# Grouped-query attention: V of the second K/V unit asked for ahead of its K, and VectorE's share of the exponentials also in chunk 3

## The chip, the cores and the metric

One core of one Trainium2 chip. The metric is the device time of one execution in microseconds (us). The span of the profile, from the first instruction to the last, is 1.6 to 1.8 us shorter than the device time. Three words recur: a transfer is *issued* when SyncE begins to put it into its queue (the profile gives how long that holds SyncE), it *lands* when its last byte is announced, and the *fill* is the first 12 us or so, until TensorE runs without a gap.

## The reference

Softmax attention in bfloat16, 16 batches, 32 query heads on 8 K/V heads (4 query heads share one), 288 queries, 512 keys, 128 columns per head:

```python
B, Hq, Hkv, Sq, Sk, D = 16, 32, 8, 288, 512, 128
scores = jnp.einsum("bhqd,bhkd->bhqk", q, k) * scale
p = _softmax(scores, axis=-1)
return jnp.einsum("bhqk,bhkd->bhqd", p, v)
```

## The kernel before

A group is one K/V head of one batch with its 4 x 288 = 1152 queries: 128 groups. A group is cut into 3 chunks of 1536 columns of transposed scores, so 384 chunks. For chunk n TensorE makes the scores (`ps_s`), ScalarE their exponentials (`pt_sb`), TensorE, two chunks behind, the product with V (`ps_o`), with a column of ones that gives the row sums, and VectorE divides and evicts (`rl_sb`, `o_sb`). In a "shared" chunk, each sixth one, VectorE makes 120 of the 1536 exponentials with a bit trick and a polynomial: `y`, `t`, `m`, `e`, three times `u`, and the result into `pt_sb`, eight operations in all.

```python
    UG = 4                      # groups in one K/V unit: one transfer of K and one of V for four groups
    SHARED = list(range(2 * NC, NS - NC, EVERY)) + [NS - NC]      # NC = 3, EVERY = 6, NS = 384
    ...
        def op_k(u, g0=0, g1=UG):                                 # K: a transposing transfer
            ...
            eng.dma_start_transpose(
                kt_sb[:, sl, :, g0:g1].rearrange("d j g p -> d j (g p)"),
                k_v[(u * UG + g0) * P:(u * UG + g1) * P]
            ).then_inc(sem["us_k%d" % sl if u > 0 else "s_k%d" % g0], 16)
    ...
        def op_vc(g):                    # GpSimd copies V beside the column of ones
            eng = nc.gpsimd
            waits = [have("v", g)]
            if g >= 2:
                waits.append(("s_pv", NC * (g - 2) + 2))
            emit(eng, waits, lambda: eng.tensor_copy(
                v_sb[:, sl, gi * NJ:(gi + 1) * NJ, 0:D], vd_sb[:, sl, gi].rearrange("p (j d) -> p j d", d=D))
            ).then_inc(sem["s_vc"], 1)
    ...
        first = [lambda: op_q0(0), lambda: op_v(0, None, 0, 1)]
        first += [lambda: op_q(1), lambda: op_k(0, 1, 2), lambda: op_v(0, None, 1, 2), lambda: op_k(0, 2),
                  lambda: op_q(2), lambda: op_v(0, None, 2, UG), lambda: op_q(3)]
        sp = []                          # the order in which SyncE issues the rest: sorted by t
        for u in range(1, NU):
            t = max(NC * UG * (u - NSLOT + 1) + 0.5, NC * (UG * u - 2.5) / AHEAD - 0.2)
            sp.append((t, lambda u=u: op_k(u)))
            sp.append((t + (2.0 if u >= NSLOT else 0.35), lambda u=u: op_v(u)))
        for g in range(UG, NG):
            t = max(NC * (g - NQ + 1) + 1.2, NC * (g - 2.5) / AHEAD)
            sp.append((t, lambda g=g: op_q(g)))
        ...
        sp.sort(key=lambda x: x[0])
    ...
            for n in range(NS):          # TensorE
                op_s(n)
                if shared(n):
                    op_sy(n)
                if n >= LAG:             # LAG = 2
                    op_pv(n - LAG)
```

All loads and stores but the first K go through SyncE's one queue. Unit 1 (groups 4 to 7) is first needed by the scores of chunk 12 (K, and Q of group 4) and by the output matmuls of chunk 12 (V, after GpSimd's copy).

Of the kernel before, what the change touches and what calls it, by code (L numbers as in the profile page):

```python
# [131 lines left out]
def bass_standalone__gqa_softmax__near_ridge_kernel(  # L132
# [19 lines left out]
    NC = COLS // CH  # L152
# [10 lines left out]
    EVERY = 6  # L163
# [5 lines left out]
    NSLOT = 3  # L169
# [6 lines left out]
    NO = 12  # L176
    NS = NG * NC
    LASTG = NG - 1
    SHARED = list(range(2 * NC, NS - NC, EVERY)) + [NS - NC]
    FINE = NG - 2  # L180
    ALONE = 8 * TPC

# [7 lines left out]
    with ExitStack() as es:  # L190
# [72 lines left out]
        def need(eng, waits):  # L263

            left = []
            for (s, n) in waits:
                key = (id(eng), s)
                if seen.get(key, 0) < n:
                    seen[key] = n
                    left.append((sem[s], n))  # L270
            return left
# [15 lines left out]
        def op_k(u, g0=0, g1=UG):  # L287
            eng = nc.sync
            sl = u % NSLOT
            if u >= NSLOT:  # L290
                for (s, n) in need(eng, [("s_s", NC * UG * (u - NSLOT + 1))]):
                    eng.wait_ge(s, n)
# [5 lines that stand above are left out]
        def op_v(u, eng=None, g0=0, g1=UG):  # L298
            eng = eng or nc.sync
            sl = u % NSLOT  # L300
            if u >= NSLOT:
                for (s, n) in need(eng, [("s_vc", UG * (u - NSLOT + 1))]):
                    eng.wait_ge(s, n)
            eng.dma_start(
                vd_sb[:, sl, g0:g1], v_v[:, u * UG + g0:u * UG + g1]
            ).then_inc(sem["us_v%d" % sl if u > 0 else "s_v%d" % g0], 16)
# [222 lines left out]
        def shared(n):  # L529
            return n in SHARED  # L530

        def nth(n):
            return SHARED.index(n) + 1

# [104 lines left out]
        sp = []  # L639
        for u in range(1, NU):  # L640
            t = max(NC * UG * (u - NSLOT + 1) + 0.5, NC * (UG * u - 2.5) / AHEAD - 0.2)
            sp.append((t, lambda u=u: op_k(u)))
            sp.append((t + (2.0 if u >= NSLOT else 0.35), lambda u=u: op_v(u)))
        for g in range(UG, NG):
            t = max(NC * (g - NQ + 1) + 1.2, NC * (g - 2.5) / AHEAD)
            sp.append((t, lambda g=g: op_q(g)))
# [124 lines left out]
```

## Time and profile before

| | |
|---|---|
| time, median of 3 runs | 521.99 us (521.82 to 522.11) |
| profiled execution | 521.84 us, span 520.2 us |
| busy: TensorE, ScalarE, VectorE, GpSimd | 99%, 99%, 71%, 15% |
| chain that ended last | TensorE 97% of the span |
| distance between chunks in the steady part | 1.33 us, for TensorE and ScalarE alike |

The page gives busy time and share per engine. The chain of waits gives, in order of time, the pieces of work that the end depended on. The timeline gives start, length, engine, line, operation, output<-inputs, shape, count, and in brackets the idle time before it and what ended that. The lines that carry the argument stand in the prediction. Two more are needed for all comparisons below, because they separate the start from the rest: the first exponential and the last reciprocal of VectorE, from the timeline of the kernel before:

```profile
4.84 1.08 ACT L521 ACTIVATE pt_sb<-ps_s 128x512 bf16<-128x512 f32 x2 [2.11 <-PE ps_s L449]
...
517.27 0.17 DVE L585 RECIPROCAL rl_sb<-ps_s 128x3 f32<-128x3 f32 x1
```

The time between them, 517.27 - 4.84 = 512.43 us, I call **the stretch**. It doesn't count the moment at which the first Q landed. It isn't wholly free of it, though: the later transfers don't wait for the first exponential, so a late start gives them a lead over the computing.

### The profile page before, as it was taken

The page shows a single profiled execution, that of the slowest core. Times are in us where ns is not written, and L with a number is a line of the kernel's source. Part 1 is how long each engine was busy: PE and PEld are TensorE (multiplying, and loading weights), DVE is VectorE, ACT ScalarE, POOL GpSimd, SP SyncE. Part 2 cuts the span into 40 slices and gives each one's busy share as a digit, 9 for nine tenths or more (in the row PEclk, how much of TensorE's full clock was granted, in tenths as well). Part 3 has the DMA queues.
Part 4 walks back from the last instruction along what each step waited for, and adds up shares of the span by engine and source line. Part 5 has one row for each costly group of instructions (what it writes and reads, how often), then busy time and mean ns, then how long its engine had stood idle before and what let it go on. Part 6 is the DMA issues. An engine that isn't in the chain of part 4 may idle for free.

```text
span 520.2 us, 15366 instructions
## 1 busy us (share of the span) xinstructions
PE 516.2 (99%) x6226; PEld 394.6 (76%) x6226; DVE 370.5 (71%) x1322; ACT 513.4 (99%) x393; POOL 79.8 (15%) x135
## 2 busy tenths in 40 slices
PE   9999999999999999999999999999999999999997
PEld 5777777777777777777777777777777777777776
DVE  2767767777777677676776776767767767777777
ACT  7999999999999999999999999999999999999997
POOL 1111111111111111111111111111111111111110
PEclk9999999999999999999999999999999999999999
DMA  8999999899999998999999999999999999998212
GB/s 167 211 234 269 257 206 250 213 205 223 212 228 263 220 240 203 225 240 240 223 235 211 201 235 215 246 191 190 230 241 238 230 205 184 198 216 221 84 69 93
DMA packets 253782, 110.06 MB, mean 212 GB/s; under 512 B 220304, under 2 KB 237584, under 8 KB 253712
## 3 DMA queue, kind: packets, MB, share of 16 engines
q1 hardware_dynamic: 253568, 108.95, 99.5%
q8 instruction: 49, 0.80, 0.7%
q14 instruction: 21, 0.17, 0.1%
q10 hardware_dynamic: 144, 0.13, 0.1%
HBM read 16.91 MB, written 37.75 MB: 105 GB/s over the span
## 4 chain that ended last, share of the span: by engine, by line
PE 97%; DVE 2%; ACT 1%; issue 0%
PE ps_o L489 49%; PE ps_s L449 46%; PE ps_o L460 1%; ACT pt_sb L521 1%; ACT pt_sb L526 1%; PE ps_o L427 0%; DVE o_sb L595 0%; DVE u_sb L559 0%; DVE rl_sb L585 0%; DVE m_sb L550 0%; PE ps_s L427 0%; DVE pt_sb L566 0%; PE ps_o L414 0%; DVE t_sb L543 0%; DVE o_sb L605 0%
## 5 line engine op out<-in xcount | busy, mean ns | idle before, releaser
L526 ACT ACTIVATE pt_sb<-ps_s 128x1536 bf16<-128x1536 f32 (+2 forms) x384 | 508.2, 1438 | 0.1
L489 PE MATMUL ps_o<-v_sb,pt_sb 128*128 128x129 bf16 x4584 | 322.6, 220 | 0.1
L489 PEld LDWEIGHTS ps_o<-v_sb,pt_sb 128*128 128x128 bf16 x4584 | 282.6, 98 | 50.2 <-DVE o_sb L595 14.1
L449 PE MATMUL ps_s<-qt_sb,kt_sb 128*128 128x512 bf16 (+2 forms) x1536 | 308.9, 324 | 0.2
L595 DVE TENSOR_TENSOR o_sb<-ps_o,rl_sb 128x384 bf16<-128x384 f32 x382 | 211.7, 554 | 8.8
L449 PEld LDWEIGHTS ps_s<-qt_sb,kt_sb 128*128 128x128 bf16 x1536 | 123.6, 98 | 61.9 <-ACT pt_sb L526 0.7
L585 DVE RECIPROCAL rl_sb<-ps_o 128x3 f32<-128x3 f32 x382 | 67.8, 178 | 128.6 <-PE ps_o L489 127.2
L578 POOL COPY v_sb<-vd_sb 128x512 bf16<-128x512 bf16 x128 | 78.8, 616 | 429.2 <-PE ps_o L489 407.6
L559 DVE SCALAR_TENSOR_TENSOR u_sb<-u_sb,m_sb 128x120 f32<-128x120 f32 x128 | 36.2, 283 | 2.2
L566 DVE SCALAR_TENSOR_TENSOR pt_sb<-u_sb,e_sb 128x120 bf16<-128x120 f32 x64 | 18.1, 283 | 2.3
L559 DVE SCALAR_TENSOR_TENSOR u_sb<-m_sb 128x120 f32<-128x120 f32 x64 | 17.7, 276 | 0.0
L537 DVE TENSOR_SCALAR y_sb<-ps_o 128x120 f32<-128x120 f32 x64 | 16.2, 253 | 0.0
L550 DVE TENSOR_SCALAR m_sb<-t_sb 128x120 int32<-128x120 int32 x64 | 14.6, 228 | 2.2
L460 PE MATMUL ps_o<-qt_sb,kt_sb 128*128 128x120 bf16 x64 | 13.8, 216 | 0.0
L550 DVE TENSOR_SCALAR e_sb<-t_sb 128x120 int32<-128x120 int32 x64 | 13.8, 216 | 0.0
L543 DVE TENSOR_SCALAR t_sb<-y_sb 128x120 int32<-128x120 f32 x64 | 13.7, 214 | 0.0
L460 PEld LDWEIGHTS ps_o<-qt_sb,kt_sb 128*128 128x128 bf16 x64 | 6.3, 98 | 7.7 <-DVE o_sb L595 0.3
L521 ACT ACTIVATE pt_sb<-ps_s 128x512 bf16<-128x512 f32 (+1 forms) x6 | 4.3, 748 | 2.1 <-PE ps_s L449 2.1
L621 DVE TENSOR_REDUCE st_sb<-rl_sb 128x1 f32<-128x72 f32 (+1 forms) x16 | 3.4, 215 | 0.0
L623 DVE TENSOR_REDUCE st_sb<-rl_sb 128x1 f32<-128x72 f32 (+1 forms) x16 | 3.4, 215 | 0.0
L427 PE MATMUL ps_o<-const-bfloat16-1.0 128*128 128x512 bf16 (+1 forms) x6 | 2.4, 573 | 0.9 <-PEq L756 0.9
L685 ACT ACT_TABLE_LOAD x1 | 1.3, 1283 | 1.2 <-PEq L756 1.2
(32 smaller groups left out, 11.7 us busy)
## 6 DMA issues: line engine op xcount, KB each, us to landing
out_dram<-o_sb SPq DMA_DIRECT2D x126, 288.0 KB, 4.0
vd_sb<-in_v_dram SPq DMA_DIRECT2D x31, 512.0 KB, 5.4
qt_sb<-in_q_dram SPq DMA_TRANSPOSE x128, 5.1
out_dram<-o_sb SPq DMA_DIRECT2D x6, 96.0 KB, 1.8
kt_sb<-in_k_dram SPq DMA_TRANSPOSE x33, 5.1
vd_sb<-in_v_dram SPq DMA_DIRECT2D x2, 128.0 KB, 3.0
vd_sb<-in_v_dram SPq DMA_DIRECT2D x1, 256.0 KB, 3.5
kd_sb<-in_k_dram ACTq DMA_DIRECT2D x1, 128.0 KB, 2.3
```

The source lines that it names most:

```text
L449: ins = emit(eng, w_x, lambda: eng.matmul(ps_s[:, n % 2, c:c + w], kt_sb[:, sl, j, gi, :], qg[:, t * P:t * P + w], start=True, stop=True))
L460: emit(eng, [("s_ev", n - LAG - 1)], lambda: eng.matmul(ps_o[:, (n - LAG) % 2, BANK - W:BANK], kt_sb[:, (g // UG) % NSLOT, j, g % UG, :], ...
L489: ins = emit(eng, w_x, lambda: eng.matmul(outs(r)[:, t - r % NC * TPC, :], pt(g, t, j), v_sb[:, sl, gi * NJ + j, 0:DV], start=(x == 0), st ...
L526: emit(eng, waits, lambda: eng.activation(d, s, ACTF.Exp, scale=scale)).then_inc(sem["s_e"], 1)
L537: emit(eng, [("s_yb", nth(n) - NB), ("s_pv", n - LAG + 1)], lambda: eng.tensor_scalar(out=y_sb[:, b], in0=ps_o[:, (n - LAG) % 2, BANK - W: ...
L543: emit(eng, [("s_ym", 2 * (nth(n) - NB)), ("s_y", nth(n))], lambda: eng.tensor_scalar(out=t_sb[:, b], in0=y_sb[:, b], scalar1=Y_MUL, scala ...
L550: emit(eng, [("s_yp", nth(n) - NB), ("s_yb", nth(n))], lambda: eng.tensor_scalar(out=dst[:, b], in0=t_sb[:, b], scalar1=mask, scalar2=bits ...
L559: lambda: eng.scalar_tensor_tensor(out=u_sb[:, b, x], in0=src, scalar=QUARTIC[x], in1=m, op0=ALU.add, op1=ALU.mult)
L566: lambda: eng.scalar_tensor_tensor(out=pt_sb[:, n % NPT, CH - W:CH], in0=u_sb[:, b, 2], scalar=QUARTIC[3], in1=e_sb[:, b].bitcast(FP32), o ...
L578: emit(eng, waits, lambda: eng.tensor_copy(v_sb[:, sl, gi * NJ:(gi + 1) * NJ, 0:D], vd_sb[:, sl, gi].rearrange("p (j d) -> p j d", d=D))). ...
L585: emit(eng, [("s_pv", r + 1)], lambda: eng.reciprocal(rl_sb[:, TPC * r:TPC * (r + 1)].unsqueeze(2), outs(r)[:, :, D:DV])).then_inc(sem["s_ ...
L595: emit(eng, waits, lambda: eng.tensor_tensor(out=o_sb[:, g % NO, t0:t0 + TPC, :], in0=outs(r)[:, :, 0:D], in1=rl_sb[:, TPC * r:TPC * (r + ...
```

## The change

The intent: VectorE takes its share also in chunk 3, where ScalarE is still the limit; and V of unit 1 comes early enough for GpSimd to copy it at quiet moments, not across VectorE's work for shared chunk 12.

```diff
-    SHARED = list(range(2 * NC, NS - NC, EVERY)) + [NS - NC]
+    SHARED = [NC] + list(range(2 * NC, NS - NC, EVERY)) + [NS - NC]
@@
             sp.append((t, lambda u=u: op_k(u)))
-            sp.append((t + (2.0 if u >= NSLOT else 0.35), lambda u=u: op_v(u)))
+            sp.append((t + (2.0 if u >= NSLOT else -0.05 if u == 1 else 0.35), lambda u=u: op_v(u)))
```

The second line changes the order of three transfers from K of unit 1, Q of group 4, V of unit 1 to V, K, Q.

## The prediction

> **What bounds the kernel now.** I read the page first: its busy shares and the chain that ended last.
>
> ```profile
> PE 516.2 (99%) x6226; PEld 394.6 (76%) x6226; DVE 370.5 (71%) x1322; ACT 513.4 (99%) x393; POOL 79.8 (15%) x135
> ...
> PE 97%; DVE 2%; ACT 1%; issue 0%
> ```
>
> TensorE (PE) and ScalarE (ACT) are both busy 99% of the 520.2 us span, but 97% of the chain that sets the end is TensorE. VectorE (DVE) has 29% of idle time on average. So a change can only pay where the chain leaves TensorE, and the short shares "DVE 2%; ACT 1%" say that this is little. To find where they lie I read the chain in order of time, first from 4 to 16 us:
>
> ```profile
> 6.41 0.92 ACT pt_sb L521
> 7.33 0.49 ACT pt_sb L526
> 7.82 0.92 ACT pt_sb L521
> 8.74 1.84 ACT pt_sb L526 x2
> 10.58 0.05 issue
> 10.63 0.83 PE ps_s L449 x6
> ```
>
> Each row is start, length, engine and tile. From 4.84 to 10.58 us the chain runs through ScalarE's exponentials: in the fill, scores are there before ScalarE gets to them, and TensorE's next score matmuls (10.63) wait for the exponential of chunk 3 to free a score buffer. The last one of the pair in "x2" is chunk 3: chunks 0, 1 and 2 are cut into 3, 2 and 2 pieces, and I counted them off. After 12 us the chain is all TensorE, until a second excursion near 22 us (the same view, 19 to 27 us):
>
> ```profile
> 21.02 0.69 PE ps_o L489 x12
> ...
> 22.80 0.52 DVE m_sb L550
> ...
> 24.59 0.48 DVE o_sb L595
> 25.07 0.05 issue
> 25.12 0.85 PE ps_o L489 x12
> ```
>
> Here TensorE waits until VectorE has evicted an output. That chunk is number 12, a "shared" one, in which VectorE does 120 of the 1536 exponentials per partition. One operation stands out: m_sb took 0.52 us, while the page's group of that form has a mean of 228 ns. Why, the timeline shows. GpSimd (POOL) and VectorE around it, and below them the same operations in chunk 6, the shared chunk before it:
>
> ```profile
> 22.07 1.17 POOL L578 COPY v_sb<-vd_sb 128x512 bf16<-128x512 bf16 x2 [7.68 <-DMA vd_sb<-in_v_dram]
> ```
>
> ```profile
> 21.73 0.18 DVE L585 RECIPROCAL rl_sb<-ps_o 128x3 f32<-128x3 f32 x1 [0.56 <-PE ps_o L489]
> 22.80 0.52 DVE L550 TENSOR_SCALAR m_sb<-t_sb 128x120 int32<-128x120 int32 x1
> 24.51 0.55 DVE L595 TENSOR_TENSOR o_sb<-ps_o,rl_sb 128x384 bf16<-128x384 f32 x1
> ```
>
> ```profile
> 13.75 0.18 DVE L585 RECIPROCAL rl_sb<-ps_o 128x3 f32<-128x3 f32 x1 [0.63 <-PE ps_o L489]
> 14.73 0.22 DVE L550 TENSOR_SCALAR m_sb<-t_sb 128x120 int32<-128x120 int32 x1
> 16.15 0.55 DVE L595 TENSOR_TENSOR o_sb<-ps_o,rl_sb 128x384 bf16<-128x384 f32 x1
> ```
>
> GpSimd waited 7.68 us for V of the second unit (groups 4 to 7) and then copied groups 4 and 5 back to back, 22.07 to 23.24, straight across VectorE's integer work. m_sb began at 22.80, and its follower at 23.24, the moment the copies ended. From the reciprocal to the start of the second eviction it took 24.51 - 21.73 = 2.78 us in chunk 12 and 16.15 - 13.75 = 2.40 us in chunk 6: 0.38 us lost. What TensorE felt of it is the distance between score chunks:
>
> ```profile
> 22.86 0.82 PE L449 MATMUL ps_s<-qt_sb,kt_sb 128*128 128x512 bf16 x6
> 24.20 0.81 PE L449 MATMUL ps_s<-qt_sb,kt_sb 128*128 128x512 bf16 x3
> 25.12 0.85 PE L489 MATMUL ps_o<-v_sb,pt_sb 128*128 128x129 bf16 x12
> ```
>
> Chunks follow each other every 1.33 us (22.86 to 24.20 is 1.34), but the one after 24.20 begins at 25.81: 1.61, so **0.28 us** are lost. Note what V's lateness itself costs: nothing. The copy of group 4 ended about 22.7, and the first matmul that reads it begins at 23.52.
>
> **What the Trainium skill says.** "SBUF — State Buffer", section "Who interferes with whom": VectorE and GpSimd share one pair of ports as an exclusive lock; tensor_scalar in a two-port mode, or a VectorE instruction with two SBUF inputs beside a GpSimd instruction that reads SBUF, blocks until the other is done. The trace agrees: m_sb, SBUF to SBUF, stretched from 0.22 to 0.52 us and the next operation started with the end of the copies, while the eviction out of PSUM at 22.00 kept its 0.55 us under them. "ScalarE: Activation LUTs", section "What ACT_TABLE_LOAD costs", has 0.833 ns per element of an activation's width; the chain above has 0.49 us for 512 and 0.92 for 1024 columns, 0.84 ns per column. "DMA: Bandwidth & Descriptors", section "Queues, rings and completion order": descriptors of one queue are consumed in ring order on each DMA engine. The landings below keep the order of issue, so I count with a first-in-first-out queue.
>
> **The change, part by part.**
> (1) Chunk 3 becomes shared. Its exponential shrinks from 1536 to 1416 columns: 120 x 0.84 ns = **0.10 us** less on ScalarE, at 8.74 to 10.58, where ScalarE is the chain. TensorE's 10.63 and the later wait for chunk 4 (a gap of 0.18 us before the row at 11.96 in the timeline) both move 0.10 earlier, and from there TensorE runs without a gap, so the shift stays to the end. TensorE gets one more matmul of 120 columns and one shorter by as much: the chain has 0.60 + 0.05 us for a shared chunk's scores against 0.65 for another: 0. VectorE gets seven operations, by the page's means 253 + 214 + 228 + 216 + 276 + 2 x 283 + 283 ns = 2.04 us, from about 9.3 to 11.8, in time that was partly idle (0.69 and 0.56 us of gaps there). Taking chunk 6's length, the second eviction would end near 9.23 + 2.95 = 12.2 us instead of 11.3; the first matmul that needs the buffer, in chunk 6's scores, comes at 12.75 (0.10 earlier now). 0.4 us of room, so cost 0. GpSimd copies at 8.62 to 9.24 and again from 12.92: no overlap.
> (2) V of unit 1 goes ahead of its K. Before, SyncE's issues:
>
> ```profile
> 11.21 3.28 SPq L293 DMA_TRANSPOSE kt_sb<-in_k_dram  x1
> 14.53 2.53 SPq L313 DMA_TRANSPOSE qt_sb<-in_q_dram  x1
> 17.10 0.58 SPq L304 DMA_DIRECT2D vd_sb<-in_v_dram  x1
> ```
>
> K landed 6.8 us after issue (18.0), Q of group 4 after 4.4 (18.9), V after 4.8 (21.9). With V first, V is issued at 11.2 and should land at about 15.5 to 18. GpSimd then copies group 4 when its other condition holds (the output matmuls of chunk 7, over at 17.7) and group 5 after chunk 10 (21.7), as in steady state. A single copy of 0.62 us from 21.75 ends at 22.4, under the PSUM operations and before the t_sb operation (22.46). The 0.28 us stall goes: **-0.28 us**.
> The price: K and Q of group 4 stand behind 512 KB. The first score matmul that needs both starts at 20.20 (0.10 earlier now), so Q's room is 20.1 - 18.9 = 1.2 us. Issue alone delays them by 0.6. The bytes take some 1.3 us at the 400 GB/s that the windows show around 21 us, where V and a store moved; in a strict queue Q lands at 20.2 and costs 0.1. But between 15 and 17 us the windows show only 65 and 91 GB/s: the queue was not full, and part of V's time falls into such holes. My estimate is Q at 19.6, with a third of a chance that TensorE waits, by 0.1 to 0.6 us. Expected cost: **+0.05**.
> Sum: 521.99 - 0.10 - 0.28 + 0.05 = 521.66, say 521.65 us.
>
> **The rivals.**
> (a) K or Q of unit 1 becomes the new wait. For it: the queue argument above, 1.2 us of room against 0.6 to 1.4 of delay. Against it: the holes at 15 to 17 us. In the worst case, Q landing at 21, 0.9 us are lost and the kernel takes 522.5.
> (b) Nothing moves: V was hidden anyway and ScalarE's fill is swallowed. For it: no matmul waited for V, and later evictions still make weight loads wait for VectorE (62 waits, 14.1 us together). Against it: those waits repeat each sixth chunk and cost no period, as 1.33 us is kept there, while the 0.28 us gap is a single one. It would make 522.0.
> (c) VectorE's extra work at 9 to 12 us becomes the bound of the fill: for it, ScalarE's gain is only 0.10 us; against it, 0.4 us of room. If wrong, 0.1 to 0.3 us are lost: 522.0.
> (d) The gain is larger because a shared chunk gives ScalarE a lead. Against it: from 12 us on TensorE is the chain without a gap, so a lead is of no use.
>
> **Range and chances.** The largest sum that the profile allows is 0.38 us, 0.07% of the time; the largest loss I can construct is about 1 us. Runs before differ by 0.3 us (521.82 to 522.11). So: 521.65 us, range 521.2 to 522.2; faster by over 2% (below 511.6) 0.005, within 2% 0.99, slower by over 2% 0.005.
>
> **What would show it.** Right: one GpSimd copy at about 17.7 and one at 21.7, no wait for V beyond; m_sb near 0.22 us in every shared chunk; score chunks 1.33 us apart through 20 to 26 us; score matmuls at 10.53 instead of 10.63; the chain in time without VectorE after 12 us. Wrong: a wait of TensorE for K or Q at about 20.1 (rival a), an output matmul near 12.7 that waits for an eviction (rival c), or a profile with all this and yet the same time, which would mean that run-to-run noise covers 0.3 us.

## The result, and the profile after

| | median | lowest to highest | runs |
|---|---|---|---|
| before | 521.90 us | 521.82 to 522.11 | 6 |
| changed | 521.96 us | 521.86 to 522.91 | 6 |

The ratio is 1.0005, with a 95% interval of 0.9992 to 1.0018. A ratio here is the mean time of one kernel's runs over that of the other's of the same rounds, so it is not quite the ratio of the medians. The time lies in the range, but the gain of 0.34 us that was forecast isn't there; three later jobs with the changed kernel gave means 0.34, 0.35 and 0.62 us above before.

From the page of the changed kernel, busy shares and the chain that ended last:

```profile
PE 510.8 (98%) x6121; PEld 394.8 (76%) x6227; DVE 371.8 (71%) x1330; ACT 513.2 (99%) x393; POOL 79.8 (15%) x135
...
PE 97%; issue 1%; DVE 1%; DMA 1%
```

(Some matmul records are missing: 6121 beside 6227 weight loads.) Nothing has changed at this scale, except that a transfer now has a share in the chain. The chain in order of time shows which:

```profile
0.82 3.88 DMA qt_sb<-in_q_dram
...
4.75 2.67 PE ps_s L449 x12
...
11.08 0.83 PE ps_s L449 x6
```

In this execution the very first Q landed at 4.70 us, against 4.37 before, although nothing ahead of it had changed. The first exponential came 0.55 us later (the other 0.22 us go with TensorE's clock, see "The start" below), and the row that I had predicted at 10.53 is at 11.08: 11.08 - 5.39 = 5.69 us after the first exponential, where before it was 10.63 - 4.84 = 5.79. The 0.10 us of chunk 3 are there. From the timeline of the changed kernel, the same two marks as before (x1 in place of x2 only because this view's window ends within the pair):

```profile
5.39 0.60 ACT L521 ACTIVATE pt_sb<-ps_s 128x512 bf16<-128x512 f32 x1 [2.67 <-PE ps_s L449]
...
517.44 0.17 DVE L585 RECIPROCAL rl_sb<-ps_s 128x3 f32<-128x3 f32 x1
```

The stretch is 517.44 - 5.39 = 512.05 us: 0.38 less than before, to the hundredth what the two parts promised without a price (0.10 + 0.28). And GpSimd's copies of groups 4 and 5, and m_sb in chunk 12:

```profile
18.22 0.62 POOL L578 COPY v_sb<-vd_sb 128x512 bf16<-128x512 bf16 x1 [3.25 <-PE ps_o L489]
...
22.21 0.62 POOL L578 COPY v_sb<-vd_sb 128x512 bf16<-128x512 bf16 x1 [3.38 <-PE ps_o L489]
...
23.16 0.22 DVE L550 TENSOR_SCALAR m_sb<-t_sb 128x120 int32<-128x120 int32 x1
```

They are apart, wait for TensorE and not for V, and m_sb has its 0.22 us again. The score chunk that came 1.61 us after its predecessor now comes at the usual distance (24.65 to 25.97):

```profile
24.65 0.81 PE L449 MATMUL ps_s<-qt_sb,kt_sb 128*128 128x512 bf16 x3
...
25.97 0.81 PE L449 MATMUL ps_s<-qt_sb,kt_sb 128*128 128x512 bf16 x3
```

So this profile shows the mechanism whole, and the time shows no gain. SyncE's issues show a first hint of why:

```profile
11.34 0.57 SPq L304 DMA_DIRECT2D vd_sb<-in_v_dram  x1
11.96 4.08 SPq L293 DMA_TRANSPOSE kt_sb<-in_k_dram  x1
16.08 2.46 SPq L313 DMA_TRANSPOSE qt_sb<-in_q_dram  x1
```

With V ahead of it, the issue of K takes 4.08 us, not 3.28. Q of group 4 is issued 1.5 us later than before and, with 4.4 us to landing, lands at 20.5: 15.10 us after the first exponential. The scores that need it begin 0.16 later. This run got through, and it did so because its start was late: counted from the start of the span, Q landed at 20.49 us here and at 20.56, 20.15 and 21.39 in the three later traces of the same kernel, whose first exponentials were at 4.94, 4.82 and 5.18. With the first exponential at 4.84, as in the kernel before, 20.49 would have been 15.65 after it, and TensorE would have waited, if the transfers moved as they did.

### The profile page after: what moved, and what is told of

Same layout as the page of the kernel before. It is cut to its first block, busy times and chain, and to the rows that moved or that the text cites. A ratio compares the mean times of both kernels' runs of the same rounds, so it can differ in the third digit from the quotient of the medians.

```text
span 520.2 us, 15272 instructions
## 1 busy us (share of the span) xinstructions
PE 510.8 (98%) x6121; PEld 394.8 (76%) x6227; DVE 371.8 (71%) x1330; ACT 513.2 (99%) x393; POOL 79.8 (15%) x135
## 4 chain that ended last, share of the span: by engine, by line
PE 97%; issue 1%; DVE 1%; DMA 1%
PE ps_o L489 50%; PE ps_s L449 46%; DMA qt_sb<-in_q_dram 1%; PE ps_o L460 1%; DVE o_sb L595 0%; DVE u_sb L559 0%; DVE rl_sb L585 0%; DVE o_sb L605 0%; DVE pt_sb L566 0%; DVE t_sb L543 0%; PE ps_o L677 0%; DVE m_sb L550 0%; DVE bad_sb L631 0%; DVE flag_i L738 0%; DVE y_sb L537 0%
## 5 line engine op out<-in xcount | busy, mean ns | idle before, releaser
L449 PE MATMUL ps_s<-qt_sb,kt_sb 128*128 128x512 bf16 (+2 forms) x1430 | 290.1, 320 | 4.8 <-DMA qt_sb<-in_q_dram 0.3
L550 DVE TENSOR_SCALAR m_sb<-t_sb 128x120 int32<-128x120 int32 x65 | 14.5, 223 | 2.2
```

Source lines behind the costliest of these rows:

```text
L449: ins = emit(eng, w_x, lambda: eng.matmul(ps_s[:, n % 2, c:c + w], kt_sb[:, sl, j, gi, :], qg[:, t * P:t * P + w], start=True, stop=True))
L550: emit(eng, [("s_yp", nth(n) - NB), ("s_yb", nth(n))], lambda: eng.tensor_scalar(out=dst[:, b], in0=t_sb[:, b], scalar1=mask, scalar2=bits ...
```

## The experiments

Theories. **A**: the gain is real, but the start varies more than the gain and hides it. **B**: the change makes the start late. **C**: the one queue is a race: V ahead of K makes Q of group 4 late in some executions, as V behind K is late in some. **D**: the gap in chunk 12 had another cause than GpSimd's copies. In each trace I took the first exponential, the stretch, and the landings of Q of group 4 and V of unit 1 counted from the first exponential (issue plus time to landing). All results were correct. In all thirteen traces the reciprocal of chunk 18 and the last one are 484.40 or 484.41 us apart, so every difference in the stretch below arises in the first 29 us after the first exponential.

| kernel, profiled execution | time | first exp. | Q lands | V lands | stretch |
|---|---|---|---|---|---|
| before | 521.84 | 4.84 | 14.13 | 17.11 | 512.43 |
| before, again | 522.74 | 4.94 | 14.57 | 18.55 | 513.28 |
| before, third | 521.69 | 5.08 | 14.19 | 15.85 | 512.14 |
| changed | 522.01 | 5.39 | 15.10 | 11.02 | 512.05 |
| changed, again | 522.11 | 4.94 | 15.62 | 12.15 | 512.46 |
| changed, third | 521.57 | 4.82 | 15.34 | 11.17 | 512.18 |
| changed, fourth | 522.91 | 5.18 | 16.22 | 12.00 | 513.07 |
| share in chunk 3 alone | 522.15 | 5.45 | 13.74 | 16.39 | 512.04 |
| V first alone | 521.65 | 4.77 | 15.43 | 12.34 | 512.28 |
| copies made to collide | 522.33 | 5.17 | 15.26 | 10.98 | 512.47 |
| K split | 521.43 | 4.82 | 13.02 | 14.55 | 512.05 |
| K split, again | 522.02 | 5.17 | 12.63 | 14.16 | 512.29 |
| K split, no share in chunk 3 | 521.51 | 4.90 | 12.05 | 13.96 | 512.15 |

### b_again and b3: the kernel before, unchanged

> The kernel before, unchanged, for the spread of its start. Theory (the gain is there, the start hides it): first exponential somewhere from 4.8 to 5.6 us by chance of the first Q transfer's landing and of the moment the TensorE clock is granted in full; from the first exponential to the last reciprocal 512.4 us as in the first profile (4.84 to 517.27). Rival (the change itself makes the start late): first exponential at 4.84 again, within 0.1.

> The kernel before a third time with a trace, for the landing of V. Theory: 512.15 from the first exponential to the last reciprocal if V lands before about 16.7 us after the first exponential, 512.43 if it lands near 17.1, and more, about one for one, beyond 18.

`b_again`, five runs: 521.79 to 522.74, mean 522.06; ratio to before's own nine runs of the job 1.0001 (0.9988 to 1.0015). The first exponential was at 4.94, so the start had changed little, yet the stretch was 513.28, 0.85 more than in the first profile of the same kernel. The expectation of a constant 512.4 was wrong. The timelines of GpSimd and TensorE show why:

```profile
23.61 1.22 POOL L578 COPY v_sb<-vd_sb 128x512 bf16<-128x512 bf16 x2 [9.04 <-DMA vd_sb<-in_v_dram]
```

```profile
24.36 0.84 PE L489 MATMUL ps_o<-v_sb,pt_sb 128*128 128x129 bf16 x12 [0.59 <-POOL v_sb L578]
25.41 0.82 PE L449 MATMUL ps_s<-qt_sb,kt_sb 128*128 128x512 bf16 x3 [0.21 <-DMA qt_sb<-in_q_dram]
```

V landed 1.4 us later after the first exponential than in the first profile, and now the output matmuls waited for the copy itself, 0.59 us: they began at 24.36, where the first profile has them at 23.52, or 23.62 with the later start, so V cost about 0.74 us. The whole loss of this execution was 1.13 (against 512.15, the stretch without late transfers, shown further down). The rest is another transfer: the scores of chunk 15 waited for Q of group 5, which is issued behind V (at 18.42) and landed after 6.9 us, at 25.37; in the first profile it was issued at 18.28 and took 5.5. Without a loss these scores would have begun at about 24.30 (24.20 in the first profile, and the start 0.10 later), so they were 1.11 late. The chain that ended last goes through this Q, from 18.42 to 25.37, and not through V: two transfers were late at once, and the later one set the end. `b3` came out as expected: V landed at 15.85 and the stretch was 512.14; five runs, mean 521.85, ratio 0.9999 (0.9986 to 1.0013). Its last clause, "about one for one, beyond 18", has `b_again` alone to support it, and there Q of group 5 hides it. So theory C's second half holds for the kernel before: with V behind K, V is late in some executions.

### a_again, a3, a4: the changed kernel, unchanged

> The changed kernel, unchanged. Theory: from the first exponential to the last reciprocal 512.05 us again (5.39 to 517.44 in its first profile), 0.38 less than before; its start varies by chance, so in five rounds against before it is 0.2 to 0.4 us faster if the first six runs were bad luck. Rival (systematically late start): first exponential again near 5.4 and the same time as before. Rival (the gain is lost later in the kernel): the duration from first exponential to last reciprocal is 512.3 or more.

> The changed kernel a third time, for the spread of Q of group 4. Theory: from the first exponential to the last reciprocal 512.05 plus what Q of group 4 lands later than 15.2 us after the first exponential; the mean time of five rounds is that of before within 0.3 us.

> The changed kernel a fourth time. Theory: 512.05 plus the lateness of Q of group 4 beyond 15.2 us after the first exponential, 0 to 0.7 us; mean time 0.2 to 0.4 us above before as in the two jobs so far.

Means of five runs and ratios: 522.15, 1.0007 (0.9993 to 1.0020); 522.10, 1.0009 (0.9996 to 1.0023); 522.52, 1.0010 (0.9996 to 1.0023); before in the same jobs 521.81, 521.75 and 521.91. Each interval holds 1, but all four jobs with the changed kernel lie on the slow side. The first expectation, 512.05 again and 0.2 to 0.4 us faster than before, was wrong: the stretch was 512.46, 512.18 and 513.07, and the mean 0.34 us slower. The stretches of `a3` and `a4` came out as their theories had them, but not the times: 0.35 above before for `a3` ("within 0.3"), 0.62 for `a4` ("0.2 to 0.4"), and the lateness of `a4` was 1.01, over the 0.7 allowed. The first exponentials at 4.94, 4.82 and 5.18, and 5.08 in before's third trace, speak against B: in the changed kernel too it was as early as in the kernel before. A is true of the start's spread, but doesn't suffice: beyond the start, the stretch loses too. In the fourth trace the loss is plain. SyncE's issues, then TensorE's scores of chunk 12:

```profile
10.96 0.58 SPq L304 DMA_DIRECT2D vd_sb<-in_v_dram  x1
11.59 5.35 SPq L293 DMA_TRANSPOSE kt_sb<-in_k_dram  x1
16.97 2.40 SPq L313 DMA_TRANSPOSE qt_sb<-in_q_dram  x1
```

```profile
21.44 0.77 PE L449 MATMUL ps_s<-qt_sb,kt_sb 128*128 128x512 bf16 x3 [0.84 <-DMA qt_sb<-in_q_dram]
```

The issue of K took 5.35 us, and TensorE waited for Q. Against 512.05, the four traces of the changed kernel lost 0.00, 0.41, 0.13 and 1.02 us, with Q landing at 15.10, 15.62, 15.34 and 16.22: beyond about 15.21 it is one for one (15.62 - 15.21 = 0.41, 15.34 - 15.21 = 0.13, 16.22 - 15.21 = 1.01). (The 15.21 is taken from the second trace; the third and the fourth test it.) From its own issue to its landing Q took 4.4, 3.7, 4.4 and 4.4 us, before 4.4, 5.3 and 4.7: what delays it is that K, issued behind V, holds SyncE for 4.1 to 5.4 us in place of 3.0 to 3.3. The transfers have holes there. Stretches of 1 us of the fourth trace (busy time and instructions per engine, granted clock, DMA share, GB/s):

```profile
15.00:16.00 1.00, 1.00 (x16) 0.76 (x14) 0.96 (x6) 1.00 (x2) 0.00 (x0) 1.00 2.45 111
16.00:17.00 1.00, 1.00 (x14) 0.66 (x12) 0.96 (x4) 1.00 (x2) 0.00 (x0) 1.00 0.14 30
...
18.00:19.00 1.00, 1.00 (x14) 0.76 (x13) 0.72 (x2) 1.00 (x2) 0.61 (x1) 1.00 0.12 7
```

Two holes, 15 to 17 and 18 to 19 us. In the kernel before there was one (65 and 91 GB/s from 15 to 17), in the first profile of the changed kernel also one (7 GB/s from 17 to 18). What makes them was not tested. The packed traces have one 16 KB fetch of instructions each in that time: at 14.7, 14.3 and 15.6 us in the three of the kernel before, at 16.3, 14.5, 16.1 and 17.5 in the four of the changed one; the emptiest stretch of 1 us (65, 2 and 30 GB/s; 7, 69, 18 and 7 GB/s) begins 0.3 to 1.5 us after it in all seven. That speaks for the fetch as a cause, but no run moved it alone, and the first hole of the fourth trace has no fetch before it.

### share3 and vfirst: each part alone

`share3` has only the first line of the diff, `vfirst` only the second.

> Only VectorE's share in chunk 3; V stays behind K. Theory: 0.10 us off the stretch from first exponential to last reciprocal (512.33), and the 0.28 us gap of TensorE in chunk 15 stays, with an integer operation of VectorE at about 0.5 us in chunk 12. Rival (VectorE's extra work costs something at 12 us): 512.43 or more.

> Only V of the second unit ahead of its K; chunk 3 stays with ScalarE. Theory: 0.28 us off the stretch from first exponential to last reciprocal (512.15), no gap of TensorE between 20 and 26 us. Rival (K or Q of group 4 comes too late): a wait of TensorE for a transfer at about 20 us and 512.3 or more.

`share3`: mean 521.83, ratio 0.9999 (0.9985 to 1.0012); stretch 512.04, not 512.33: the 0.10 us are there, and the gap of 0.28 us isn't, although V stayed behind K. V landed at 16.39 after the first exponential, because this execution's start was late (5.45) and the transfers had caught up; both copies were over at 23.12, ahead of m_sb at 23.23, and the operation before it was stretched by 0.02 only (0.23 for 0.21). `vfirst`: mean 522.16, ratio 1.0009 (0.9995 to 1.0023); stretch 512.28 in place of 512.15, without a gap of TensorE later on. Q landed at 15.43 and TensorE lost 0.13. With ScalarE 0.10 later in this kernel, the need is at 15.31 and the lateness 0.12. So in the traces the second part, not the first, brings the loss; the times point the same way, but neither interval excludes 1.

### collide: the contention made again in the changed kernel

```diff
+            if g == UG:
+                waits.append(("s_y", 3))      # copy of group 4 only after VectorE has begun shared chunk 12
```

> The changed kernel, but GpSimd's copy of group 4 waits until VectorE has done its first operation for the shared chunk 12, so that the copies of groups 4 and 5 run back to back across VectorE's integer and polynomial work although V landed long before. Theory (the port, not the transfer, made the gap of 0.28 us): one or more of VectorE's SBUF-to-SBUF operations of chunk 12 take 0.4 us or more instead of 0.22 to 0.28, and TensorE's score chunks after it show a gap of 0.2 to 0.6 us. Rival (the gap came from the transfers that moved at that time): no operation stretched, no gap there.

One run, 522.33 us, of unknown state. V had landed 6.3 us before, and still, from the timelines of GpSimd, VectorE and TensorE:

```profile
22.45 1.17 POOL L580 COPY v_sb<-vd_sb 128x512 bf16<-128x512 bf16 x2 [7.75 <-DVE y_sb L537]
```

```profile
23.17 0.52 DVE L550 TENSOR_SCALAR m_sb<-t_sb 128x120 int32<-128x120 int32 x1
```

```profile
25.49 0.85 PE L489 MATMUL ps_o<-v_sb,pt_sb 128*128 128x129 bf16 x12 [0.18 <-DVE o_sb L597]
```

m_sb is back at 0.52 us and its predecessor took 0.37 in place of 0.21; the score chunks at 24.50 and 26.18 are 1.68 us apart. From the reciprocal of chunk 10 to the last one it took 0.35 us more than in the changed kernel's first profile (517.64 - 22.04 against 517.44 - 22.19). D falls: the copies' time alone makes the gap; V had long landed. (The whole stretch, 512.47, is 0.42 above that first profile. The other 0.07 or 0.08 us were lost before chunk 10, by a late clock, see `ksplit2` below; it also fits that Q, at 15.26, was not waited for.)

### ksplit, ksplit2 and ksplit_noshare: both races taken away

If the order of 512 KB blocks is a race that one of them loses, the cure is not another order but a smaller first piece. K of group 4 (128 KB) goes first, then Q of group 4, V of the unit, and then K of groups 5 to 7, which chunk 15 needs:

```diff
-            ).then_inc(sem["us_k%d" % sl if u > 0 else "s_k%d" % g0], 16)
+            ).then_inc(sem["s_k4" if (u, g1) == (1, 1) else "us_k%d" % sl if u > 0 else "s_k%d" % g0], 16)
@@  have()
+            if (kind, g) == ("k", UG):
+                return ("s_k4", 16)
@@
-            sp.append((t, lambda u=u: op_k(u)))
-            sp.append((t + (2.0 if u >= NSLOT else -0.05 if u == 1 else 0.35), lambda u=u: op_v(u)))
+            if u == 1:
+                sp.append((t, lambda u=u: op_k(u, 0, 1)))
+                sp.append((t + 0.4, lambda u=u: op_k(u, 1, UG)))
+            else:
+                sp.append((t, lambda u=u: op_k(u)))
+            sp.append((t + (2.0 if u >= NSLOT else 0.35), lambda u=u: op_v(u)))
```

`ksplit` and `ksplit2` are this on the changed kernel; `ksplit_noshare` has SHARED as before.

> The changed kernel with K of unit 1 asked for in two parts: group 4 alone first (128 KB), then Q of group 4, then all of V, then K of groups 5 to 7. Theory (the one queue is a race: whichever of Q and V stands behind the 512 KB of the other is late): Q of group 4 lands at least 0.5 us before the 15.2 us after the first exponential at which its matmul comes, V lands before 16.8, so neither gap shows, and from the first exponential to the last reciprocal it is 512.05, within 0.05; in five rounds 0.2 to 0.6 us faster than before. Rival (the landings are late for another cause, such as the instruction fetch near 15 us): Q at 15.4 or V at 17 all the same, 512.3 or more.

> The version with K of unit 1 split and the share in chunk 3, again. Theory: 512.05 from the first exponential to the last reciprocal, Q of group 4 landed before 14.5 and V before 16.5 us after the first exponential; mean time 0.15 to 0.5 us below before. Rival (its first five rounds were luck): the mean of before within 0.1.

> K of unit 1 split as in the run that had no late landing, but chunk 3 stays with ScalarE whole. With both races taken away it measures the share of chunk 3 alone. Theory: from the first exponential to the last reciprocal 512.15, 0.10 more than with the share; 0.1 us slower in the rounds than the same kernel with the share, which the spread of the start may hide. Rival (the share is worth nothing without late transfers): 512.05.

SyncE's issues in `ksplit`:

```profile
11.24 1.26 SPq L293 DMA_TRANSPOSE kt_sb<-in_k_dram  x1
12.54 1.43 SPq L313 DMA_TRANSPOSE qt_sb<-in_q_dram  x1
14.02 0.58 SPq L304 DMA_DIRECT2D vd_sb<-in_v_dram  x1
```

K of one group is issued in 1.26 us, Q 2 us earlier than before. Q landed at 13.02, 12.63 and 12.05, V at 14.55, 14.16 and 13.96 in the three traces: about 2 us of room each. No transfer was waited for in any of them. The stretch was 512.05 with the share and 512.15 without it: the share of chunk 3 is worth 0.10 us, measured with nothing late. `ksplit2` had 512.29 where 512.05 was expected. There the trace records the full TensorE clock only from 6.80 us on (`ksplit`: 4.42), and already the first reciprocal came 3.30 us after the first exponential in place of 2.93. (These moments are the clock records of the packed trace; the column of granted clock shows 1.00 before the first record too, because time without a record is counted as full.) In `collide`, with the full clock from 6.37, it was 3.09; in the nine other traces that have such a record, all from 5.86 or earlier, 2.93. So a clock that comes after about 6 us goes with a longer stretch, which was seen and not tested.

The times: 521.59 mean against 521.75 before, ratio 0.9998 (0.9984 to 1.0011); 521.81 against 521.91, 0.9997 (0.9983 to 1.0010); without the share 521.62 against 521.91, 0.9995 (0.9981 to 1.0008). The forecasts of a gain of 0.2 to 0.6 (`ksplit`) and of 0.15 to 0.5 us (`ksplit2`) were both missed: 0.16 and 0.10, and for `ksplit2` the rival, before's mean within 0.1, came in. All three means lie below before's and below those of the changed kernel in their jobs (522.10; 522.52 for the last two), but no interval excludes 1: it is the best version found, not a proven gain over the kernel before. Against the changed kernel the difference is larger: ten runs of `ksplit` and `ksplit2` have a mean of 521.70, ten of `a3` and `a4` in the same jobs 522.31, and no run of the ten is above 522.02, while eight of the other ten are. `ksplit_noshare` being ahead of `ksplit2` in the times, against the traces, shows how far the start blurs 0.1 us.

### ksplit_vact: a second queue for the first V

`ksplit`, and V of group 0 issued from ScalarE's queue.

```diff
-        first = [lambda: op_q0(0), lambda: op_v(0, None, 0, 1)]
+        first = [lambda: op_q0(0)]
@@  ScalarE
             op_kd(eng)
+            op_v(0, eng, 0, 1)
```

> As the one before, and V of group 0 is issued by ScalarE's queue at the start, so that SyncE issues everything after the first Q 0.6 us earlier. Theory: 512.05 again with all landings earlier by 0.4 to 0.6 us; first Q lands later by up to 0.3 us because 128 KB more move beside it, and the first exponential with it; so no gain in time over the run before. Rival: the first Q is not touched, and the same time as the run before within 0.1.

Median 523.57, mean 523.77, ratio 1.0035 (1.0022 to 1.0049). A miss. The first scores, from TensorE's timeline:

```profile
6.61 2.81 PE L451 MATMUL ps_s<-qt_sb,kt_sb 128*128 128x512 bf16 x8 [2.30 <-DMA qt_sb<-in_q_dram]
```

The expectation's "no gain" held, its sizes didn't. The first Q, issued at 0.82 as ever, landed at 6.57 in place of 4.35 in `ksplit`, and the 128 KB of V beside it at 6.4, 5.2 us after their issue. I had allowed for 0.3 us. In the meantime the trace has TensorE's clock back at half, from 7.45 to 10.87 us, and the stretch was 512.83. The later landings were indeed earlier on the clock, which was of no use. Besides V, the second Q was issued 0.6 us earlier too (2.25 in place of 2.87); which of the two held up the first Q was not separated.

## Why the prediction came out as it did

- **Chunk 3's share, -0.10 us**: right, on ScalarE's chain and without a cost at 12 us. `share3` (512.04), and `ksplit` against `ksplit_noshare` (512.05 and 512.15) show it. Rival (c), VectorE's extra work as a bound, and rival (d), a larger gain by a lead, found no support. ("Seven operations" is a slip for eight; the sum of 2.04 us has all eight.)
- **The gap of 0.28 us by GpSimd's copies**: the mechanism was right; `collide` makes it again by the copies' time alone, with m_sb at 0.52 us and not 0.22. The size was one draw: in three traces of the kernel before V landed at 17.11, 18.55 and 15.85, and cost 0.28, about 0.74 and 0.00 us (the second lost 1.13, by Q of group 5, which stood behind V). I took a single profile's gap for a constant.
- **"Expected cost: +0.05" for Q**: this is the term that failed. It rested on "a third of a chance that TensorE waits, by 0.1 to 0.6 us" and on V's bytes filling the holes between 15 and 17 us. Measured in four traces of the changed kernel, with a loss in three: 0.00, 0.41, 0.13 and 1.02 us, 0.39 in the mean, eight times my figure. I put Q at 19.6; it landed at 20.49, 20.56, 20.15 and 21.39. My delay of 0.6 us for the issue counted V's own issue alone; K's issue, which I left at 3.28 us, grew to between 4.08 and 5.35, so Q was issued 1.2 to 2.4 us later than the 14.53 of before. Nor did V's bytes go into the holes: the emptiest microsecond now lay between 16 and 19 us, around V's landing or behind it. (The "400 GB/s" is not in the windows either: they have 364 and 374, which makes 512 KB 1.4 us and not 1.3.) That is rival (a), to which I gave too little.
- **The start**: left out altogether. The first exponential was at 4.77 to 5.45 us in the traces of kernels whose first transfers are alike, with the first Q landing between 4.30 and 4.77. It followed this landing by 0.47 us in the traces with the full clock by 4.44, and by 0.68 or 0.69 in those with it from 5.27 or later. A term of 0.68 us of spread belonged beside a gain of 0.34. The 0.3 us between the runs before, which I did quote, was too few runs to show it. On one half of it the Trainium skill has a word: "TensorE: Matmul & The Clock Gate", section "Part 1: The HAM clock gate (the 'warmup' mystery)", says that the window after which the full clock is granted is free-running, so that the moment varies from run to run; the traces agree, with full clock recorded from 4.02 to 6.80 us on in eleven traces (two have no record).
- **Range and chances**: the time, 521.96, was inside 521.2 to 522.2, and within 2% was right. That was luck: the sum was carried by a term of +0.05 that measures several times that. The time is also the 522.0 of rival (b), but (b) held that nothing moves, and the traces show two terms that did.

The change thus trades one late transfer for another. V's lateness goes (with what stood behind it 0.28, 1.13 and 0.00 us), Q's comes (0.00, 0.41, 0.13, 1.02), and the 0.10 us of chunk 3 remain, under a start that varies by 0.68. The traced executions alone don't say which is dearer: their mean stretch is 512.62 before and 512.44 changed, and one of the three before was the slowest of all its kernel's runs. The runs without a trace say more. Pooled over all jobs, 21 runs of the changed kernel have a mean of 522.23 us and 43 of the kernel before 521.87, from four jobs on different chips, so this is rough. An estimate: device time less first exponential less stretch is at most 4.71 us in the thirteen traces, the latest first exponential is 5.45, and a late clock cost up to 0.24. A run with no late transfer should then take at most 5.45 + 512.05 + 0.24 + 4.71 = 522.45 us changed and 522.55 before. Above that lie 5 of the 21 and 1 of the 43 (the traced 522.74). So large losses seem more frequent with V ahead of K.

What stays open: how often the smaller losses occur in the runs without a trace, what makes the holes in the transfers, and why the issue of K varies between 4.08 and 5.35 us behind V.

## What to carry to other kernels

When one queue feeds a kernel's fill, putting one large transfer ahead of another moves the wait; ask which later transfer inherits the delay, count its issue time as well as its bytes, and make the first piece as small as its first user needs before changing the order. A gain that one profile shows, by the lateness of one transfer, is one draw: take the same profile three times before putting a number on it. For effects below 1 us, measure from the first exponential to the last result, so that the start doesn't hide them, and look at the landings as well: a late start can hide a late transfer.

## What the Trainium skill lacked or had wrong

- "DMA: Bandwidth & Descriptors", "Issuing engines are not separate DMA queues": it says that such transfers interleave on the same DMA engines and that issuing from several only saves the sequencer's time. Here it cost: with 128 KB of plain load from ScalarE's queue (V of group 0) beside a transposing load from SyncE's, the latter landed at 6.57 us in place of 4.35 (the next transposing load was issued 0.6 us earlier, too, so the share of each is open). A delay fits the interleaving; what the page lacks is a figure for a transposing load that shares the engines with another queue.
- The same page gives no figure for how long a large transposing load holds the engine that issues it. Here 128 KB took 1.26 us and 256 KB 1.23 in the fill, 512 KB from 2.97 to 3.28 us behind other transposes and from 4.08 to 5.35 behind 512 KB of plain load, and this, not the bytes, set when the next load began.
- "TensorE: Matmul & The Clock Gate", "Part 1: The HAM clock gate": it puts the spread of the full clock's beginning at ±500 ns from run to run. The clock records of eleven traces here have 4.02 to 6.80 us after the span's start, with TensorE's first matmul at about 0.9 in each, a range of 2.8 us, in kernels whose first 4 us are alike.
